# Second layer of a gated feed-forward block: a seven-product form over pairs of quad pairs in two of three passes

## The chip, the cores and the metric

One core of a Trainium2 chip runs the whole program. The metric is device time in microseconds (us), the median of repeated runs; less is better. Line numbers (L1168 and so on) are those of the kernel before, unless it says "of the changed kernel".

## What is computed

Three layers in a row on 2304 tokens of width 512: pooled attention, a mixture of eight experts, and a gated layer. The change touches the gated layer only:

```python
def _moe2_ref(x, w_gate, w_val, w_out):       # x: 2304 x 512, w_gate and w_val: 512 x 1536, w_out: 1536 x 512
    g = x @ w_gate
    silu = g * (1.0 / (1.0 + np.exp(-g)))
    val = x @ w_val
    return (silu * val @ w_out).astype(np.float32)
```

The multiplication by `w_gate` and `w_val` is called the first layer here, that by `w_out` the second.

## The kernel before

**Numbers.** Each operand of a matmul is split into a high part, rounded to the matmul's input type, and a low part, the rest. One product is then three matmuls: high by high, high by low and low by high (`mm3`, L117 to L119, and L1168 to L1170 in the second layer).

**Passes and quads.** Tokens are worked on in three passes of `TB` = 768 (two halves of `HB` = 384). The loop over `m` at the end of the program is the gated layer: 18 steps, six for each pass (`SP2` = 6), and each step takes 256 of the 1536 hidden columns. A step has two calls of `quad`, one with gate weights and one with value weights. A quad is the 256 hidden columns by 768 tokens of the first layer in a form of Strassen's: seven products M1 to M7 of two halves each, so 42 matmuls of 384 columns, in the order M1, M2, M5, M6, M7, M4, M3. Their sums are taken in part in PSUM: M1, M6, M7 and M4 add up in one tile `a` (named `aps`), M5 and M3 in `c` (`cps`), M2 is in `b` (`bps`). After M1, M6 and M7 the running sum in `a` is copied out by ScalarE (ACT, `part_sum`, L1097), and the next product then adds on to the same tile. VectorE (DVE) makes the four blocks 11, 22, 21 and 12 of the result from these copies.

**Second layer.** Before, a step's gated block (silu times value, split in high and low by `value_sink`) is multiplied with the 256 rows of `w_out` by `second_tile`: six token tiles for each step, six matmuls of 512 columns for each tile, into `yps`. They are not run at once: the tiles of step m are queued in `ys` and handed out by `fill_y` within the two quads of step m + 1, three to each, two of them between M6 and M7 and one between M7 and M4. DVE adds each tile to an accumulator in `AC` (L1663); in the sixth step of a pass the tile is then stored. After the last step six tiles are left, and end the program.

**Who sets the order.** The program is written in the order in which it is to run; each engine takes its instructions in that order and waits on semaphores. `quad` calls `after` behind each product: it runs what is in `late` (work of the next engine in a chain), the product's sink, the tasks put at that point (`tasks`) and one step of `side`. PSUM has eight banks: before, in this stage, two for `a`, one for `b`, two for `c` and three for `yps`.

**Rows of w_out.** They are split in high and low once, in the first pass, stored in DRAM (`rows_d`) and fetched by a DMA of GpSimd's queue (POOL) in the later passes, twelve times 1 MB (`split_rows`, L853).

The expert stage ahead of this one already has its second layer as seven products over pairs of quads (`block`, into `mbs`, 128x384 matmuls). Its blocks stand at several points of each quad, among them between M6 and M7 (`at_block`).

## Time and profile before

| | us |
|---|---|
| median of 3 runs | 1985.78 |
| lowest and highest run | 1985.34, 1986.54 |
| the profiled execution's own time | 1986.16 |
| its span, first to last instruction | 1984.5 |

The profile is of one execution, so a sum made from its rows is set against 1986.16, which is 0.38 us over the median. PE is TensorE's matmuls, PEld its weight loads, SPq the queue that issues most DMAs. A matmul's row lasts longer than the stretch to the next matmul's start, because matmuls are pipelined: what one costs in a stream is read as the distance from start to start. Columns of the rows below: a row of the timeline is start and length in us, engine, line, operation, output and input tile, shapes, and in brackets the idle time before it and who ended it. A row of stretches is the stretch, its length, the busy us (and instructions) of PE, PEld, DVE, ACT and POOL, the granted clock as a share of 2.4 GHz, the busy share of the DMA engines and GB/s. A row of groups is line, engine, operation, tiles, shapes and count, then busy us and mean ns of one, then the idle time before them. The gated layer lies from about 1570 us to the end, its passes two and three from about 1705 us.

### The profile page before, as it was taken

How to read it: one execution, taken by the hardware profiler on the slowest of the kernel's cores; microseconds unless marked ns; L12 is line 12 of the kernel's file. 1: busy time of each engine (PE TensorE's matmuls, PEld its weight loads, DVE VectorE, ACT ScalarE, POOL GpSimd, SP SyncE). 2: the span in 40 equal slices, each digit the busy share in tenths (PEclk: the TensorE clock that was granted, in tenths of full speed). 3: DMA queues.
4: the chain of work that ended last, by engine and by line, in shares of the span. 5: the costliest groups of instructions: out<-in, count | busy, mean ns of one | idle time of the engine just before them, and what ended most of it. 6: DMA issues, size and time to landing. Idle time of an engine off the chain costs nothing.

```text
span 1984.5 us, 31152 instructions
## 1 busy us (share of the span) xinstructions
PE 1964.2 (99%) x11081; PEld 1871.4 (94%) x11081; DVE 1421.9 (72%) x2257; ACT 885.8 (45%) x1709; POOL 1310.0 (66%) x1173
## 2 busy tenths in 40 slices
PE   8999999999999999999999999999999999999999
PEld 7899888999999899999999999999999999999998
DVE  7763868777777868877777788777776855656555
ACT  4453544444444444443444434444444554544543
POOL 7674567888887466867667667677675766445442
PEclk9999999999999999999999999999999999999999
DMA  7674677888888899989989899898888564543542
GB/s 195 183 210 117 218 274 267 311 292 311 312 304 307 295 315 320 330 300 313 313 306 316 292 309 330 312 312 310 314 318 284 174 239 149 201 161 138 173 146 85
DMA packets 217227, 513.82 MB, mean 259 GB/s; under 512 B 35472, under 2 KB 107760, under 8 KB 210928
## 3 DMA queue, kind: packets, MB, share of 16 engines
q1 hardware_dynamic: 212176, 496.10, 72.8%
q0 software_dynamic: 4896, 15.73, 2.9%
q8 instruction: 88, 1.44, 0.3%
q14 instruction: 67, 0.55, 0.1%
HBM read 360.73 MB, written 151.04 MB: 258 GB/s over the span
## 4 chain that ended last, share of the span: by engine, by line
PE 92%; DVE 4%; DMA 1%; ACT 1%; issue 1%; POOL 1%; SPq 0%; DVEq 0%; POOLq 0%; ACTq 0%
PE aps L119 8%; PE aps L117 8%; PE aps L118 8%; PE mbs L118 7%; PE mbs L117 7%; PE mbs L119 7%; PE yps L1168 6%; PE yps L1170 6%; PE yps L1169 6%; PE cps L117 4%; PE cps L119 4%; PE cps L118 4%; PE bps L117 2%; PE bps L118 2%; PE bps L119 2%; PE mps L360 1%
## 5 line engine op out<-in xcount | busy, mean ns | idle before, releaser
L1097 ACT COPY LF<-aps 128x384 f32<-128x384 f32 x378 | 181.5, 480 | 439.6 <-PE aps L119 437.4
L1329 POOL TENSOR_TENSOR LR<-LF,LR 128x384 fp32r<-128x384 f32 x240 | 261.0, 1110 | 172.7 <-ACT LR L1327 172.6
L117 PE MATMUL mbs<-LR 128*128 128x384 f32 x840 | 283.1, 337 | 0.0
L118 PE MATMUL mbs<-LR 128*128 128x384 f32 x840 | 282.5, 336 | 0.0
L119 PE MATMUL mbs<-LR 128*128 128x384 f32 x840 | 281.9, 336 | 0.0
L1376 DVE TENSOR_TENSOR AC<-mbs,AC 128x768 f32<-128x768 f32 x196 | 187.1, 955 | 131.8 <-PE mbs L119 131.1
L1168 PE MATMUL yps<-LR 128*128 128x512 f32 x576 | 225.7, 392 | 0.2 <-DVE AC L1428 0.2
L1170 PE MATMUL yps<-LR 128*128 128x512 f32 x576 | 225.2, 391 | 0.5 <-DVE LR L1611 0.5
L1169 PE MATMUL yps<-LR 128*128 128x512 f32 x576 | 224.6, 390 | 0.2 <-POOL LR L66 0.2
L846 POOL TENSOR_TENSOR LR<-praw,LR 128x512 fp32r<-128x512 f32 (+1 forms) x130 | 135.9, 1064 | 108.4 <-ACT LR L840 68.5
L846 POOL TENSOR_TENSOR LR<-sums,LR 128x1024 fp32r<-128x1024 f32 x65 | 159.2, 2449 | 68.1 <-ACT LR L840 68.1
L1342 POOL TENSOR_TENSOR LF<-LF 128x384 f32<-128x384 f32 x120 | 129.1, 1075 | 57.2 <-DVE LF L1496 45.4
L118 PEld LDWEIGHTS mbs<-LR 128*128 128x128 f32 x840 | 157.8, 188 | 0.0
L119 PEld LDWEIGHTS mbs<-LR 128*128 128x128 f32 x840 | 157.7, 188 | 0.0
L117 PEld LDWEIGHTS mbs<-LR 128*128 128x128 f32 x840 | 157.6, 188 | 0.0
L1430 DVE SCALAR_TENSOR_TENSOR AC<-yps,pr,AC 128x512 f32<-128x512 f32 x168 | 121.1, 743 | 30.9 <-PE yps L1170 27.0
L1336 ACT COPY LF<-bps 128x384 f32<-128x384 f32 x120 | 57.7, 481 | 185.9 <-DVE bps L1496 182.3
L1346 POOL TENSOR_TENSOR LF<-LF 128x384 f32<-128x384 f32 x120 | 130.5, 1088 | 9.4
L1170 PEld LDWEIGHTS yps<-LR 128*128 128x128 f32 x576 | 108.1, 188 | 24.4 <-DVE LR L1611 1.0
L66 POOL TENSOR_TENSOR LR<-rraw,LR 128x512 fp32r<-128x512 f32 x72 | 99.2, 1397 | 41.1 <-ACT LR L65 37.8
L1168 PEld LDWEIGHTS yps<-LR 128*128 128x128 f32 x576 | 108.2, 188 | 19.1 <-DVE AC L1428 0.7
L1169 PEld LDWEIGHTS yps<-LR 128*128 128x128 f32 x576 | 108.2, 188 | 18.5 <-POOL LR L66 0.6
(320 smaller groups left out, 5743.1 us busy)
## 6 DMA issues: line engine op xcount, KB each, us to landing
LR<-w1s_d SPq DMA_DIRECT2D x210, 512.0 KB
LR<-w2s_d SPq DMA_DIRECT2D x210, 512.0 KB
w1s_d<-LR SPq DMA_DIRECT2D x29, 1792.0 KB
w2s_d<-LR SPq DMA_DIRECT2D x24, 1024.0 KB
w2s_d<-LR SPq DMA_DIRECT2D x90, 256.0 KB
praw<-in_moe_w_dram SPq DMA_DIRECT2D x30, 512.0 KB
rraw<-in_moe_w_dram SPq DMA_DIRECT2D x30, 512.0 KB
LR<-rows_d POOLq DMA_DIRECT2D x12, 1024.0 KB, 7.3
```

What stands on the lines that cost most here:

```text
L117: nc.tensor.matmul(ps, lhsT=wh, rhs=ah, start=start, stop=False, skip_group_check=more)
L118: nc.tensor.matmul(ps, lhsT=wh, rhs=al, start=False, stop=False, skip_group_check=more)
L119: nc.tensor.matmul(ps, lhsT=wl, rhs=ah, start=False, stop=stop, skip_group_check=more)
L846: nc.gpsimd.tensor_tensor(out=lo, in0=src, in1=hi.bitcast(F32), op=ALU.subtract)
L1097: nc.scalar.copy(out=t, in_=ps[:, :HB])
L1168: nc.tensor.matmul(ps, lhsT=hh[:, o:o + P], rhs=wh, start=j == 0, stop=False)
L1169: nc.tensor.matmul(ps, lhsT=hh[:, o:o + P], rhs=wl, start=False, stop=False)
L1170: nc.tensor.matmul(ps, lhsT=hl[:, o:o + P], rhs=wh, start=False, stop=j == 1)
L1329: eng.tensor_tensor(out=lo[:, c], in0=src[:, c], in1=hi[:, c].bitcast(F32), op=ALU.subtract)
L1342: nc.gpsimd.tensor_tensor(out=r_of(q, a), in0=r_of(q, b), in1=r_of(q, a), op=ALU.subtract)
L1346: nc.gpsimd.tensor_tensor(out=r_of(q, a), in0=r_of(q, a), in1=r_of(q, b), op=ALU.subtract)
L1376: nc.vector.tensor_tensor(out=acc_of(m), in0=ps[:, :, :HB], in1=acc_of(m), op=ALU.add)
```

## The change

In passes two and three the second layer gets the seven-product form too, with the tokens stationary.

- Two steps make a pair `j` (six hidden blocks of 256 make three pairs in a pass). The gated blocks 11, 22, 21 and 12 of both steps are kept in fp32 (`r_of`), M1, M3 and M2 take a block as it is (`pair_sink`, `split_b`), the other four take sums (`sum_t13`, `sum_t24` on DVE, `split_t` on ACT and POOL).
- `gated_block` is one of the seven products of a pair: 18 matmuls of 256 columns (three token tiles, two steps, three of a split product) into a tile `mbs` of two banks. DVE adds it to `AC` (768 columns).
- The blocks of pair j stand in the four quads of pair j + 1, seven points in all (`at_gated`): after M7 of each quad, and after M2 of all but the first of the four. The last seven run at the end.
- The weight sets of the seven products are made in pass one (`gated_row_sums` on DVE, `split_gated_sums` on ACT and POOL), stored in `w3s_d`, and streamed by SP, 512 KB a block, three blocks ahead. `rows_d` and its twelve DMAs of POOL's queue are gone.
- From the third step of pass two on, PSUM is two banks for `a`, one each for `b` and `c`, and four for two tiles `mbs`. The six tiles left from pass one are handed out two to a quad, in the first three quads of pass two.
- In pass one the low part of a gate or value set's sums is taken in two POOL instructions of 512 columns instead of one of 1024 (in all three passes of this layer, since `pair_lo` is shared).

```diff
 def pair_lo(i, what):
...
-                        nc.gpsimd.tensor_tensor(out=lo, in0=src, in1=hi.bitcast(F32), op=ALU.subtract)
+                        parts = [slice(0, 2), slice(2, 4)] if j == 2 and i >= NE else [slice(None)]
+                        for c in parts:
+                            nc.gpsimd.tensor_tensor(out=lo[:, c], in0=src[:, c], in1=hi[:, c].bitcast(F32), op=ALU.subtract)
...
-                if p:
-                    nc.gpsimd.dma_start(out=rsets[i].rearrange("p a d -> p (a d)"), in_=rows_d[:, (i - NE) % NG])
...
+        def split_gated_sums():
+            t, w = part_of(10.5, 8 * P, F32).rearrange("p (m f) -> p m f", m=4), gated_row_set()
+            nc.scalar.activation(out=w[:, :, 0], in_=t, func=AF.Copy)
+            for c in range(2):
+                m = slice(2 * c, 2 * c + 2)
+                nc.gpsimd.tensor_tensor(out=w[:, m, 1], in0=t[:, m], in1=w[:, m, 0].bitcast(F32), op=ALU.subtract)
...
+        def pair_sink(gs, q):
+            def sink(name, ps, t):
+                src = whole(name, ps, t)
+                out = gs[name] if name == "12" else src
+                nc.vector.tensor_tensor(out=out, in0=src, in1=gs[name], op=ALU.mult)
+                if name != "12":
+                    weighed[q, name] = src
+                    late.append(lambda: split_b(q, {"11": "M1", "22": "M3", "21": "M2"}[name], name))
+            return sink
...
+        GX = ("M1", "M3", "M2", "M6", "M5", "M7", "M4")
...
+        def finish(p, m, other):
+            V = nc.vector
+            return {"M1": [add_of(V, "M2", "M1"), add_of(V, "M6", "M1")],
+                    "M2": [out_rows(p, "M2", 0, 0)],
+                    "M6": [add_of(V, "M7", "M6"), add_of(other, "M3", "M6")],
+                    "M5": [add_of(other, "M3", "M5"), out_rows(p, "M3", 0, 1)],
+                    "M7": [add_of(V, "M4", "M7"), add_of(other, "M5", "M7"), out_rows(p, "M5", 1, 1)],
+                    "M4": [out_rows(p, "M4", 1, 0)]}.get(m, [])
...
+        def gated_block(v, at_once=False):
+
+            j, m = GORDER[v]
+            w = gated_set(v)
+            ps = pools["mb"].tile([P, 2, 512], F32, tag="mb", name="mbs").rearrange("p a b -> p (a b)")[:, :TB]
+            for a in range(3):
+                y = ps[:, 2 * P * a:2 * P * (a + 1)]
+                for q in range(2):
+                    hh, hl = (h[:, a * P:(a + 1) * P] for h in h_of(q, m))
+                    nc.tensor.matmul(y, lhsT=hh, rhs=w[:, q, 0], start=q == 0, stop=False)
+                    nc.tensor.matmul(y, lhsT=hh, rhs=w[:, q, 1], start=False, stop=False)
+                    nc.tensor.matmul(y, lhsT=hl, rhs=w[:, q, 0], start=False, stop=q == 1)
+            load_gated(v + 3)
+            if j % NGP == 0:
+                nc.vector.tensor_copy(out=rows_of(m), in_=ps)
+            else:
+                nc.vector.tensor_tensor(out=rows_of(m), in0=ps, in1=rows_of(m), op=ALU.add)
...
+        at_gated = {(0, "M7"): 0, (1, "M2"): 1, (1, "M7"): 2, (2, "M2"): 3, (2, "M7"): 4, (3, "M2"): 5, (3, "M7"): 6}
+
+        def pair_tasks(m, x, tasks):
+
+            j = (m - SP2) // 2
+            for (a, point), k in at_gated.items():
+                if a == x and j > 0:
+                    merge(tasks, {point: [lambda k=k: gated_block(7 * (j - 1) + k)]})
+            V, G = nc.vector, nc.gpsimd
+            if x in (0, 2) and (x or j):
+                q = 0 if x else 1
+                merge(tasks, {"M1": [lambda: sum_t13(q, V)], "M2": [lambda: sum_t24(q, V)]})
+            if x == 3:
+                merge(tasks, {"M4": [lambda: split_t(0, "M6", "22", G)], "M3": [lambda: split_t(0, "M5", "11", G)]})
+            if x == 0 and j:
+                merge(tasks, {"M6": [lambda: split_t(1, "M6", "22", G)], "M4": [lambda: split_t(1, "M5", "11", G)]})
...
+            take = 2 if m in (SP2, SP2 + 1) else len(ys) // 2
+            more = deque(ys.popleft() for _ in range(min(take, len(ys))))
...
-            quad(i + 1, ys, tasks, value_sink(gs, hs, n))
+            if p:
+                pair_tasks(m, x + 1, tasks)
...
+            quad(i + 1, more, tasks, pair_sink(gs, g) if p else value_sink(gs, hs, n))
+            if m == SP2 + 1:
+                assert not ys
+                ps_open.close()
+                banks_c[:] = [ps_c]
+                pools["mb"] = ps_open.enter_context(tc.tile_pool(name="ps_mb2", bufs=2, **left))
...
-            ys = deque(second_tile(n, t, hs, done2) for t in range(TT))
+            if p == 0:
+                ys = deque(second_tile(n, t, hs, done2) for t in range(TT))
         while late:
             later()
-        while ys:
-            ys.popleft()()
+        sum_t13(1, nc.vector)
+        sum_t24(1, nc.vector)
+        split_t(1, "M6", "22", nc.gpsimd)
+        split_t(1, "M5", "11", nc.gpsimd)
+        while side:
+            side.popleft()()
+        for k in range(7):
+            gated_block(len(GORDER) - 7 + k, True)
```

PE's order in the gate quad of the last step. `aps` is the tile `a`; T2 is M6's operand, T3 that of M7. Before, two tiles `yps` of six matmuls each stand between M6 and M7; the end of the second of them and M7's start:

```order
L1168 MATMUL yps_18701<-LR_2662 128x512
L1169 MATMUL yps_18701<-LR_2662 128x512
L1170 MATMUL yps_18701<-LR_2662 128x512
L117 MATMUL aps_18653<-T3h_2271,LR_2662 128x384
L118 MATMUL aps_18653<-T3l_2272,LR_2662 128x384
L119 MATMUL aps_18653<-T3h_2271,LR_2662 128x384
```

In the changed kernel, the same quad, M6's second half and M7's start:

```order
L117 MATMUL aps_19030<-T2h_2269,LR_2662 128x384
L118 MATMUL aps_19030<-T2l_2270,LR_2662 128x384
L119 MATMUL aps_19030<-T2h_2269,LR_2662 128x384
L117 MATMUL aps_19030<-T3h_2271,LR_2662 128x384
L118 MATMUL aps_19030<-T3l_2272,LR_2662 128x384
L119 MATMUL aps_19030<-T3h_2271,LR_2662 128x384
```

M7's first matmul is now right behind M6's last one. This is so in 23 quads of the changed kernel, against two of the kernel before.

DVE's order at the end of the program, before: the last products' blocks 21 and 12 (`aps`, `cps`) are multiplied and split, and then the six tiles are added up.

```order
L1606 TENSOR_TENSOR aps_18745<-aps_18745,LF_2661 128x384
L1183 TENSOR_TENSOR cps_18764<-cps_18764,LF_2661 128x384
L1606 TENSOR_TENSOR cps_18764<-cps_18764,LF_2661 128x384
L1611 TENSOR_TENSOR LR_2662<-aps_18745,LR_2662 128x384
L1611 TENSOR_TENSOR LR_2662<-cps_18764,LR_2662 128x384
L1663 TENSOR_TENSOR AC_74<-yps_18835,AC_74 128x512
L1663 TENSOR_TENSOR AC_74<-yps_18844,AC_74 128x512
```

The end in the changed kernel: the last low part (L1357), four sums (L1361, L1365), and then the first of seven `mbs` tiles with the additions of the seven-product form (L1659).

```order
L1636 TENSOR_TENSOR aps_19142<-aps_19142,LF_2661 128x384
L1199 TENSOR_TENSOR cps_19184<-cps_19184,LF_2661 128x384
L1636 TENSOR_TENSOR LF_2661<-cps_19184,LF_2661 128x384
L1357 TENSOR_TENSOR LR_2662<-aps_19142,LR_2662 128x384
L1361 TENSOR_TENSOR LF_2661<-LF_2661 128x384 x2
L1365 TENSOR_TENSOR LF_2661<-LF_2661 128x384 x2
L1691 TENSOR_TENSOR AC_74<-mbs_19267,AC_74 128x768
L1659 TENSOR_TENSOR AC_74<-AC_74 128x768 x2
L1691 TENSOR_TENSOR AC_74<-mbs_19290,AC_74 128x768
L1691 TENSOR_TENSOR AC_74<-mbs_19311,AC_74 128x768
L1691 TENSOR_TENSOR AC_74<-mbs_19333,AC_74 128x768
```

The four sums and two additions of 768 columns now stand ahead of the addition that frees the second `mbs` tile.

## Rows read from the trace of the kernel before

**Rows 1.** the page: busy time of each engine.

```profile
PE 1964.2 (99%) x11081; PEld 1871.4 (94%) x11081; DVE 1421.9 (72%) x2257; ACT 885.8 (45%) x1709; POOL 1310.0 (66%) x1173
```

**Rows 2.** the view of stretches, in the expert stage.

```profile
1200.00:1300.00 100.00, 100.00 (x576) 100.00 (x575) 81.44 (x125) 41.81 (x81) 74.61 (x71) 1.00 0.90 313
```

**Rows 3.** the view of stretches: two steps each, in passes one, three and three.

```profile
1650.50:1695.50 45.00, 45.00 (x237) 41.96 (x237) 26.07 (x46) 23.87 (x46) 28.72 (x19) 1.00 0.49 154
...
1878.00:1924.00 46.00, 46.00 (x244) 43.06 (x243) 26.89 (x48) 20.84 (x42) 18.75 (x15) 1.00 0.40 138
1924.00:1970.00 46.00, 46.00 (x243) 43.05 (x242) 27.45 (x50) 18.57 (x38) 16.66 (x12) 1.00 0.29 104
```

**Rows 4.** the timeline of a value quad: last of M6, tiles, copy, M7.

```profile
1963.98 0.34 PE L119 MATMUL aps<-T2h,LR 128*128 128x384 f32 x1
...
1964.15 0.39 PE L1168 MATMUL yps<-LR 128*128 128x512 f32 x1
...
1964.35 0.48 ACT L1097 COPY LF<-aps 128x384 f32<-128x384 f32 x1
...
1966.88 0.34 PE L117 MATMUL aps<-T3h,LR 128*128 128x384 f32 x1
...
1967.92 0.39 PE L1168 MATMUL yps<-LR 128*128 128x512 f32 x1
```

**Rows 5.** the timeline of PE in an early stage with 128x256 matmuls.

```profile
101.39 0.28 PE L119 MATMUL hps<-xh,wl 128*128 128x256 f32 x1
...
102.47 0.28 PE L119 MATMUL hps<-xh,wl 128*128 128x256 f32 x1
```

**Rows 6.** the timeline of the first expert quad, PE and ACT, M6 to M4.

```profile
215.87 0.34 PE L119 MATMUL aps<-T2h,w 128*128 128x384 f32 x1
...
216.25 0.48 ACT L1097 COPY LF<-aps 128x384 f32<-128x384 f32 x1 [0.19 <-PE aps L119]
...
216.78 0.45 PE L117 MATMUL aps<-T3h,w 128*128 128x384 f32 x1 [0.57 <-ACT LF L1097]
...
217.76 0.34 PE L119 MATMUL aps<-T3h,w 128*128 128x384 f32 x1
...
218.67 0.44 PE L117 MATMUL aps<-LR,w 128*128 128x384 f32 x1 [0.57 <-ACT LF L1097]
```

**Rows 7.** the timeline of a gate quad in pass one, M6 to M7.

```profile
1585.07 0.34 PE L119 MATMUL aps<-T2h,LR 128*128 128x384 f32 x1
...
1585.50 0.48 ACT L1097 COPY LF<-aps 128x384 f32<-128x384 f32 x1 [0.40 <-PE aps L119]
...
1586.03 0.45 PE L117 MATMUL aps<-T3h,LR 128*128 128x384 f32 x1 [0.62 <-ACT LF L1097]
```

**Rows 8.** the timeline at the end: first tile, its wait, last matmul, addition.

```profile
1971.41 0.39 PE L1168 MATMUL yps<-LR 128*128 128x512 f32 x1
...
1972.35 0.40 PE L1169 MATMUL yps<-LR 128*128 128x512 f32 x1
...
1973.29 0.51 PE L1170 MATMUL yps<-LR 128*128 128x512 f32 x1 [0.55 <-DVE LR L1611]
...
1980.22 0.39 PE L1170 MATMUL yps<-LR 128*128 128x512 f32 x1
1980.65 0.69 DVE L1663 TENSOR_TENSOR AC<-yps,AC 128x512 f32<-128x512 f32 x1 [0.67 <-PE yps L1170]
```

**Rows 9.** the page: groups of instructions by line.

```profile
L1329 POOL TENSOR_TENSOR LR<-LF,LR 128x384 fp32r<-128x384 f32 x240 | 261.0, 1110 | 172.7 <-ACT LR L1327 172.6
...
L1376 DVE TENSOR_TENSOR AC<-mbs,AC 128x768 f32<-128x768 f32 x196 | 187.1, 955 | 131.8 <-PE mbs L119 131.1
...
L118 PEld LDWEIGHTS mbs<-LR 128*128 128x128 f32 x840 | 157.8, 188 | 0.0
```

**Rows 10.** the view of lines, expert stage, DVE, shapes apart.

```profile
L1183 DVE TENSOR_TENSOR bps<-cps,LF 128x384 f32<-128x384 f32 x48 | 26.9, 561 | 17.4 <-ACT LF L1097 17.4
...
L1349 DVE TENSOR_TENSOR AC<-AC 128x768 f32<-128x768 f32 x7 | 9.9, 1414 | 0.0
```

More of the change, by code (lines that the diff above doesn't have):

```diff
@@ L1230, in next_weights @@
                 at("M3", lambda: store_rows(n))
+                if not expert:
+                    at("M5", lambda: gated_row_sums(n))
+                    at("M4", split_gated_sums)
             at("M5", lambda: pair_sums(i + 1))
@@ new lines, in fused_kernel, with gated_set, load_gated, rows_of @@
+        NGP = NG // 2
+        GORDER = [(j, m) for j in range((NPASS - 1) * NGP) for m in GX]
+        def gated_set(v):
+            return part_of(60.5 + 4 * (v % 3), 8 * P).rearrange("p (q h f) -> p q h f", q=2, h=2)
+        def load_gated(v):
+            if v < len(GORDER):
+                j, m = GORDER[v]
+                nc.sync.dma_start(out=gated_set(v).bitcast(F32).rearrange("p q h f -> p q (h f)"),
+                                  in_=w3s_d[:, j % NGP, BX.index(m)])
+        def rows_of(m):
+            return AC[:, EX.index(m) * TB:(EX.index(m) + 1) * TB]
@@ new lines, in gated_block @@
+        def gated_block(v, at_once=False):
+            j, m = GORDER[v]
+            w = gated_set(v)
[10 more added lines that the diff above has]
+                nc.vector.tensor_copy(out=rows_of(m), in_=ps)
+            else:
+                nc.vector.tensor_tensor(out=rows_of(m), in0=ps, in1=rows_of(m), op=ALU.add)
+            if j % NGP == NGP - 1:
+                steps = finish(1 + j // NGP, m, nc.gpsimd if at_once else nc.vector)
+                if at_once:
+                    for f in steps:
+                        f()
+                else:
+                    side.extend(steps)
+            later()
@@ new lines, in fused_kernel @@
+        at_gated = {(0, "M7"): 0, (1, "M2"): 1, (1, "M7"): 2, (2, "M2"): 3, (2, "M7"): 4, (3, "M2"): 5, (3, "M7"): 6}
[12 more added lines that the diff above has]
+                merge(tasks, {"M6": [lambda: split_t(1, "M6", "22", G)], "M4": [lambda: split_t(1, "M5", "11", G)]})
+            if j == 0 and x == 3:
+                merge(tasks, {a: [lambda v=v: load_gated(v)] for v, a in enumerate(("M1", "M2", "M5"))})
@@ L1622, in fused_kernel @@
             gs, hs = {}, {}
-            more = deque(ys.popleft() for _ in range(len(ys) // 2))
+            x = l % 2 * 2
+            g = l % 2 if p else 0
+            take = 2 if m in (SP2, SP2 + 1) else len(ys) // 2
+            more = deque(ys.popleft() for _ in range(min(take, len(ys))))
             tasks = last_blocks(0) if m == 0 else {}
@@ L1635, in fused_kernel @@
                 merge(tasks, {"M2": [lambda n=("T1", "T3")[l - 3]: sum_x(n, nc.gpsimd)]})
-            quad(i, more, tasks, gate_sink(gs, m), 2 if m == 1 else 0)
+            quad(i, more, tasks, gate_sink(gs, m, g), 2 if m == 1 else 0)
             tasks = last_blocks(1) if m == 0 else {}
@@ L1649, in fused_kernel @@
                 merge(tasks, {"M2": [lambda n=("T2", "T4")[l - 3]: sum_x(n, nc.gpsimd)]})
-            quad(i + 1, ys, tasks, value_sink(gs, hs, n))
+            if p:
+                pair_tasks(m, x + 1, tasks)
+            more = ys
+            if m in (SP2, SP2 + 1):
+                more = deque(ys.popleft() for _ in range(min(2, len(ys))))
+            quad(i + 1, more, tasks, pair_sink(gs, g) if p else value_sink(gs, hs, n))
[4 more added lines that the diff above has]
+                pools["mb"] = ps_open.enter_context(tc.tile_pool(name="ps_mb2", bufs=2, **left))
             if m == 0:
```

73 lines of the change are left out of this document (45 added, 28 removed).

## The prediction

> **What bounds the kernel now.** I read the page first: PE is busy for 1964.2 of the span's 1984.5 us, the next engine is DVE with 72% [rows 1]. Then the stretches, because a share over the whole run can hide a stage: in passes one and three of the gated layer PE is busy in every us of 45 or 46, at clock 1.00, while ACT has 18 to 24, POOL 17 to 29 and DVE 26 to 27 [rows 3]. So in the changed stage the time is the sum of PE's start-to-start distances, plus what PE waits. A busy PE says little about the rate, so the timeline comes next, for two things: what a matmul of each width costs in a stream, and what stands between dependent products. Last the end of the program, where no other work covers a wait.
>
> **Matmuls removed and added.** The rate is read from starts. In one value quad twelve 512-column matmuls take 1966.88 - 1964.15 = 2.73 us, 0.2275 each, and six of 384 columns take 1967.92 - 1966.88 = 1.04 us, 0.1733 each [rows 4]. The 128 columns between them cost 0.054, so a line through the two forms gives 0.1733 - 0.0542 = 0.119 for 256 columns. An early stage has that form: nine of them, high and low parts mixed as in the new block, from 101.39 to 102.47 us, 0.120 each [rows 5]. I take 0.1195.
>
> Removed: 2 passes x 6 steps x 6 tiles x 6 matmuls = 432 of 512 columns, 432 x 0.2275 = 98.3 us. Added: 2 x 3 pairs x 7 products x 18 = 756 of 256 columns, 756 x 0.1195 = 90.3 us. The changed order has these counts (PE's rows grow by 324 = 756 - 432), so the change does what it says: seven eighths of the columns. The gain is **-8.0 us** and not an eighth of 98.3, because each matmul has some 12 ns that don't depend on its width, and there are more of them.
>
> **The uncovered copies.** M1, M6, M7 and M4 add up in one tile `a`, and ACT must copy `a` out before the next of them may write it. Before, two tiles `yps` stand between M6 and M7: the copy starts at 1964.35, 0.2 us behind the first tile's start, is done in 0.48 us, and M7 starts at 1966.88 without a wait [rows 4]. The change hands out its blocks after M2 and after M7, none after M6. The order shows M7 right behind M6 in 21 quads more than before: all 20 from the third step of pass two on, and the value quad of the second step, whose tiles have been used up. That quad also has nothing between M7 and M4. So 22 uncovered copies.
>
> The trace has such places. In the first expert quad the last of M6 starts at 215.87, the copy runs from 216.25, M7 starts at 216.78. The sixth matmul of M7 starts at 217.76; six undisturbed distances from 215.87 would be 216.91, so it costs 0.85 us (0.74 of wait, and about 0.11 because the first matmul after a wait is slower). M7 to M4 in the same quad is the same 0.91 from start to start [rows 6]. A gate quad of pass one, with ACT as loaded as here, has 1586.03 - 1585.07 = 0.96, a loss of 0.79, with the slow start 0.90 [rows 7]. I take 0.85: 22 x 0.85 = **+18.7 us**; bounds 22 x 0.74 = 16.3 and 22 x 0.95 = 20.9. Nothing covers it: PE takes its matmuls in order, and the wait is for the very tile it writes next. ACT is free when M6 ends (its blocks of work there, 0.5 us each, are released one or two products earlier), so I add no queueing.
>
> **The end.** Before, the six last tiles lose time once: 0.94 from 1972.35 to 1973.29, instead of 0.23, and the next 0.1 more; this goes, **-0.8**. After the last quad the new order has 7 x 18 x 0.1195 = 15.1 us of PE (counted above). Put the end of M3 at 0. DVE first finishes block 12 and the last low part (0.2 + 4 x about 0.5, done near 2), then four sums of 384, bounded below by 0.56 of the same width [rows 10] less what a read from PSUM costs, near 0.5, and above by 0.7: done near 4.2. Only then it frees the first `mbs` tile (0.96 [rows 9]): 5.2. The third block wants that tile at 4.3, and starts 0.9 late. Two additions of 768 stand next on DVE, at most 1.41 each (the row of such additions with POOL at work [rows 10]), near 1.2: 7.6; then the second tile, 8.5, wanted by the fourth block at 7.4: another 1.1. The low parts for the fourth block (ACT, then POOL with 1.11 each [rows 9]) come near 6 to 7 and are not late. So **+2.1**, bounds 0 (if the sums are done by 3.3) and 3.5. The last addition is 768 wide instead of 512 (0.96 against 0.69 [rows 8, 9]) and the last store is 384 KB beside a second one, instead of 256 KB: **+0.8**, bounds 0.3 and 1.5.
>
> **What I cost at nothing.** In pass one each step gets four additions of 256 on DVE, one ACT copy of 1024, two POOL low parts and a store in seven pieces; there DVE has 19 of 45 us free, ACT 21, POOL 16 [rows 3], and no matmul of pass one reads the result. In passes two and three SP gets 42 loads of 512 KB, each waiting for PE to finish a block, with the loads of the next weights queued behind. Three sets make a load two blocks early, at least 4 us; the DMA engines are busy for 0.29 to 0.49 there [rows 3]. Without that cover a block would wait 2 to 3 us, so up to +3 at the end, where blocks are back to back. POOL loses twelve DMA issues and gets eight low parts of 1.11 for each pair of steps: some 9 us in 48, beside 17 to 19 in 46. One `c` bank instead of two: M5 of the next quad waits for block 12. Behind a gate quad that takes three more hops (ACT, DVE), but there a block of 2.15 us stands after M2; behind a value quad it is done 1.4 us after M3, and M1 and M2 take 2.1. The expert stage lives with the same banks and has PE busy for 100 of 100 us [rows 2]. The range gets 0 to +4 for all this.
>
> **Sum.** -8.0 + 18.7 - 0.8 + 2.1 + 0.8 = +12.8. The profiled execution took 1986.16, which gives 1999.0; it is 0.4 over the median of the runs, so I say **1998.6 us**. Own bounds: -8.4 + 16.3 - 0.8 + 0 + 0.3 + 0 = +7.4, and -7.6 + 20.9 - 0.8 + 3.5 + 1.5 + 4 = +21.5.
>
> **A rule.** In the trace a weight load lasts 188 ns [rows 9], longer than the 120 ns from one 256-column matmul to the next [rows 5], so loads run under earlier matmuls and under each other. The Trainium skill, page "TensorE: Matmul & The Clock Gate", section "The mechanism", says that a weight load overlaps matmuls in flight only where it goes to another group of rows of the array. By that rule a load would stand between any two matmuls, and narrower ones would pay it more often; the trace disagrees, with its 120 ns. It stays as a rival below.
>
> **Rivals.** (1) **The copies are covered after all, and the kernel is faster.** The place is M6 to M7. Without the 18.7 the sum is -5.9, so 1979.9 us. The point from which it decides: (8.0 - 2.1) / 22 = 0.27 us for each copy. For it: PE's order leaves ACT free at that moment. Against: the copy alone takes 0.48, and all three places in the trace give 0.74 or more [rows 6, 7]. (2) **No change that can be measured**: the narrow matmuls run at their columns alone, 256 / 2.4 GHz = 0.107 us, 756 x 0.0125 = 9.5 us less, so 1989.1. Against: neither form in the stage does so [rows 4], nor did the early one [rows 5]. (3) **More waits, much slower**: with one `c` and one `b` bank and DVE in strict order, half of the 20 quads wait another 1 us behind a block's addition (0.96) at M2 or M5: +10, so 2009. For it: margins of 0.7 to 0.9 us in quads without a block after M2. Against: rows 2. (4) **Weight loads pace the blocks**: 756 x (0.188 - 0.1195) = +52, so 2051; against it stand rows 5.
>
> **How the numbers follow.** Forecast 0.80, rivals 0.05, 0.06, 0.07 and 0.02. A measurement of this kernel tells about 0.2% (4 us) from no change. Slower by more: 0.80 + 0.07 + 0.02 = 0.89; within: 0.06; faster by more: 0.05. The range holds the forecast's own bounds, 1993 to 2007, cut above where all upper ends would have to meet, and widened a little below for copies that come out shorter: 1991 to 2006. That leaves out the rivals, 2 in 10.
>
> **What will show it.** Right: in the changed profile M7's first matmul in each quad of the last 250 us waits for ACT's copy of `aps`, some 0.6 us of idle, 22 times more than before, and this group heads PE's waits; new blocks have starts 0.12 us apart; in the end the third and fourth block wait for DVE. Wrong: starts of M6's last and M7's first matmul less than 0.45 us apart, a rate of the blocks clearly off 0.12, or a larger wait than that for ACT's copy, for DVE at M2 and M5 or for a weight load.

## The result, and the profile after

| | before | after |
|---|---|---|
| time, median of 4 runs each | 1985.67 us (1985.34 to 1986.54) | 2016.05 us (2015.67 to 2017.45) |
| span of the profiled execution | 1984.5 us | 2014.0 us |
| PE, busy | 1964.2 us [rows 1] | 1965.8 us |

The changed kernel is slower: ratio 1.015, 95% interval 1.0138 to 1.0162. The prediction was 1998.6 us with a range of 1991 to 2006; direction and main mechanism hold, but the loss is more than twice the forecast. The engines' busy time on the page after answers [rows 1]:

```profile
PE 1965.8 (98%) x11405; PEld 1881.1 (93%) x11405; DVE 1494.9 (74%) x2310; ACT 909.8 (45%) x1751; POOL 1391.4 (69%) x1260
```

PE has 324 matmuls more, and its share fell by a point only. The stretches tell more. The columns are those of [rows 3] (PE, PEld, DVE, ACT, POOL busy; granted clock; DMA share; GB/s); the first three stretches are those of [rows 3], the last two are short ones behind long waits:

```profile
1650.50:1695.50 45.00, 44.15 (x233) 41.10 (x232) 35.83 (x55) 23.99 (x45) 33.08 (x26) 1.00 0.49 163
1878.00:1924.00 46.00, 42.89 (x275) 41.30 (x275) 32.53 (x51) 22.69 (x46) 24.64 (x23) 1.00 0.59 198
1924.00:1970.00 46.00, 44.05 (x290) 43.01 (x288) 28.74 (x48) 22.99 (x45) 26.19 (x24) 1.00 0.49 165
1846.00:1852.00 6.00, 4.84 (x25) 4.84 (x26) 4.39 (x7) 4.98 (x9) 4.29 (x4) 0.72 0.00 0
1994.00:2003.00 9.00, 7.94 (x53) 7.94 (x54) 7.27 (x8) 1.58 (x2) 6.14 (x5) 0.81 0.49 158
```

PE is no longer busy in every us: 2 to 3 us of 46 are idle in pass three, and 0.85 of 45 in pass one, which the forecast left untouched. DVE rose from 26 to 36 us of 45 in pass one. The clock of 0.72 and 0.81 is a mean between the two levels of 2.4 and 1.2 GHz; before, it was 1.00 in the first four, as in this one, and the program had ended ahead of the fifth:

```profile
1846.00:1852.00 6.00, 6.00 (x33) 5.64 (x32) 3.26 (x7) 2.68 (x6) 1.24 (x2) 1.00 0.66 218
```

The six largest groups of PE's waits from the start of the gated layer's pass one (line and releaser, us in total, times, longest):

```profile
PE aps L117 <- ACT LF L1113: 18.3, 24, 3.1
PE cps L117 <- DVE bps L1199: 5.1, 5, 2.1
PE mbs L1684 <- DVE AC L1691: 1.9, 1, 1.9
PE cps L117 <- DVE LF L1636: 1.0, 1, 1.0
PE mbs L1684 <- DMA LR<-w3s_d: 0.6, 1, 0.6
PE bps L117 <- DVE LF L1607: 0.5, 1, 0.5
```

The first group is the uncovered copy of the prediction: 23 of its 24 are new ([rows 7] is the 24th). Of the others only the third, a stall for DVE at the end, has a term in the forecast; the fifth, a wait for a set of weights at the end, and the rest were forecast at nothing. One ordinary place, a value quad's M6, copy, M7 and first block, against [rows 4]:

```profile
1957.47 0.34 PE L119 MATMUL aps<-T2h,LR 128*128 128x384 f32 x1
1957.85 0.48 ACT L1113 COPY LF<-aps 128x384 f32<-128x384 f32 x1 [1.76 <-PE aps L119]
...
1958.38 0.45 PE L117 MATMUL aps<-T3h,LR 128*128 128x384 f32 x1 [0.57 <-ACT LF L1113]
...
1959.53 0.28 PE L1684 MATMUL mbs<-LR 128*128 128x256 f32 x1
...
1959.65 0.28 PE L1685 MATMUL mbs<-LR 128*128 128x256 f32 x1
```

From M6's last start to M7's first there are 0.91 us, 0.74 more than the undisturbed 0.17, as in [rows 6]. The block starts are 0.12 apart, as forecast from [rows 5].

By the starts of the quads, the time went like this (us). The forecast's terms are put on the stages by their counts: -8.2 + 1.7 for steps 6 and 7 (36 matmuls of 512 columns, two copies), -81.9 + 75.3 + 17.0 for steps 8 to 17 (360 such matmuls, 630 of 256 columns, 20 copies), -8.2 - 0.8 + 15.1 + 2.1 + 0.8 for the end:

| stage | before | after | difference | in the forecast |
|---|---|---|---|---|
| pass one, steps 1 to 5 | 116.3 | 122.0 | +5.7 | 0 |
| steps 6 and 7 | 45.7 | 40.4 | -5.3 | -6.5 |
| steps 8 to 17, to the last M3's end | 228.4 | 246.4 | +18.0 | +10.4 |
| from there to the end | 13.1 | 25.3 | +12.2 | +9.0 |

### The profile page after: what moved, and what is told of

Its sections match the earlier page's. It is cut to its first block, busy times and chain, and to the rows that moved or that the text cites. A ratio compares the mean times of both kernels' runs of the same rounds, so it can differ in the third digit from the quotient of the medians.

```text
span 2014.0 us, 32218 instructions
## 1 busy us (share of the span) xinstructions
PE 1965.8 (98%) x11405; PEld 1881.1 (93%) x11405; DVE 1494.9 (74%) x2310; ACT 909.8 (45%) x1751; POOL 1391.4 (69%) x1260
## 4 chain that ended last, share of the span: by engine, by line
PE 88%; DVE 7%; ACT 2%; issue 2%; DMA 1%; POOL 0%; SPq 0%; DVEq 0%; ACTq 0%; POOLq 0%
PE aps L117 8%; PE aps L119 8%; PE aps L118 8%; PE mbs L117 7%; PE mbs L118 7%; PE mbs L119 7%; PE yps L1184 4%; PE yps L1186 4%; PE yps L1185 4%; PE cps L117 4%; PE cps L119 4%; PE cps L118 4%; PE bps L117 2%; PE bps L118 2%; PE bps L119 2%
## 5 line engine op out<-in xcount | busy, mean ns | idle before, releaser
L1348 POOL TENSOR_TENSOR LR<-LF,LR 128x384 fp32r<-128x384 f32 x288 | 314.7, 1116 | 185.1 <-ACT LR L1346 184.9
L851 POOL TENSOR_TENSOR LR<-sums,LR 128x512 fp32r<-128x512 f32 (+1 forms) x101 | 168.0, 1678 | 23.9 <-ACT LR L843 23.9
L1184 PE MATMUL yps<-LR 128*128 128x512 f32 x432 | 169.5, 392 | 0.5 <-DVE AC L1447 0.5
L1361 POOL TENSOR_TENSOR LF<-LF 128x384 f32<-128x384 f32 x120 | 129.8, 1082 | 57.2 <-DVE LF L1515 45.4
L1186 PE MATMUL yps<-LR 128*128 128x512 f32 x432 | 168.7, 391 | 0.0
L1185 PE MATMUL yps<-LR 128*128 128x512 f32 x432 | 168.3, 390 | 0.0
L1355 ACT COPY LF<-bps 128x384 f32<-128x384 f32 x144 | 69.3, 481 | 217.3 <-DVE bps L1515 183.7
L1346 ACT ACTIVATE LR<-LF 128x768 fp32r<-128x768 f32 x144 | 122.0, 848 | 48.9 <-PE mbs L119 43.2
L1365 POOL TENSOR_TENSOR LF<-LF 128x384 f32<-128x384 f32 x120 | 132.3, 1103 | 9.4
L1199 DVE TENSOR_TENSOR bps<-cps,LF 128x384 f32<-128x384 f32 x126 | 70.8, 562 | 74.8 <-ACT LF L1113 74.5
L66 POOL TENSOR_TENSOR LR<-LF,LR 128x1024 fp32r<-128x1024 f32 x24 | 60.3, 2512 | 69.2 <-ACT LR L65 63.9
L66 POOL TENSOR_TENSOR LR<-rraw,LR 128x512 fp32r<-128x512 f32 x64 | 88.5, 1405 | 28.3 <-ACT LR L65 23.9
```

The lines of the kernel that those rows point to most:

```text
L66: nc.gpsimd.tensor_tensor(out=lo, in0=src, in1=hi.bitcast(F32), op=ALU.subtract)
L851: nc.gpsimd.tensor_tensor(out=lo[:, c], in0=src[:, c], in1=hi[:, c].bitcast(F32), op=ALU.subtract)
L1184: nc.tensor.matmul(ps, lhsT=hh[:, o:o + P], rhs=wh, start=j == 0, stop=False)
L1185: nc.tensor.matmul(ps, lhsT=hh[:, o:o + P], rhs=wl, start=False, stop=False)
L1186: nc.tensor.matmul(ps, lhsT=hl[:, o:o + P], rhs=wh, start=False, stop=j == 1)
L1348: eng.tensor_tensor(out=lo[:, c], in0=src[:, c], in1=hi[:, c].bitcast(F32), op=ALU.subtract)
```

## The experiments

All kernels but the last are edits of one of the two kernels; each ran beside the kernel before, whose medians in these comparisons were 1986.1 to 1986.3 us. "Less" and "more" are against the 2016.05 of the changed kernel, or against the kernel before where that was edited. "Loss" is the distance from one matmul's start to the next above the undisturbed pitch of its width. In the traces step 1 of pass one starts anywhere from 1579.7 to 1582.5 us, so a difference of two spans holds up to 2.7 us from before that point; stages are compared where it matters.

**1. The copy alone, in the kernel before.** Its value tiles are handed out later, so that none stands between M6 and M7.

```
-            quad(i, more, tasks, gate_sink(gs, m), 2 if m == 1 else 0)
+            quad(i, more, tasks, gate_sink(gs, m), 2 if m == 1 or m >= 8 else 0)
...
-            quad(i + 1, ys, tasks, value_sink(gs, hs, n))
+            quad(i + 1, ys, tasks, value_sink(gs, hs, n), 2 if m >= 8 else 0)
```

> The kernel before with one edit: in passes two and three the waiting value tiles are not placed before the third of a quad's seven products' places (M2), so that no whole value tile stands between M6 and M7 in 20 quads; all the products stay. It makes the uncovered copy between M6 and M7 alone, without the gated layer's new second layer. Theory A: such a place costs what it costs in the changed kernel (.74 to .98 us; the prediction took .85): 20 places give 15 to 20 us, some 2002 us. Rival: in the kernel before ScalarE and VectorE are far enough ahead that a copy hides at half that price or that other tiles take up the slack: under 10 us, below 1996.

Measured: 2003.91 us (2002.36 to 2004.77), ratio 1.0091 (1.0074 to 1.0108): 17.8 us more; the profiled spans differ by 16.2. PE's waits from 1742 us on are one group:

```profile
PE aps L117 <- ACT LF L1097: 12.8, 20, 1.3
```

That is 0.81 to 0.89 us for each of the 20 places, net. By the starts of the quads, steps 8 to 17 took 18.4 us longer, 0.92 a place (one, at the start of pass three, lost 1.51), and the end took 0.8 less, because its one stall was gone. The price of the copy (0.85) and its size as the largest term are shown, apart from the new second layer.

**2. A block at M6 instead of M2.** Fifteen copies get a block of 2.15 us as cover.

```
-        at_gated = {(0, "M7"): 0, (1, "M2"): 1, (1, "M7"): 2, (2, "M2"): 3, (2, "M7"): 4, (3, "M2"): 5, (3, "M7"): 6}
+        at_gated = {(0, "M7"): 0, (1, "M6"): 1, (1, "M7"): 2, (2, "M6"): 3, (2, "M7"): 4, (3, "M6"): 5, (3, "M7"): 6}
```

> The changed kernel with one edit: the 15 blocks of gated products that stood at M2 of a quad (three for each pair of columns of the five full pairs) stand at M6, where in the kernel before a whole value tile or nothing stood. Theory A: a block at M6 covers ScalarE's copy of M6's partial sums that M7's eviction needs; each such place now costs .74 to .98 us, so 15 go: 11 to 13 us less; against it, new waits at the places where a gate quad's products now come with nothing between them (10 places of .5 to 1 us): 2008 to 2013 us. Rival: these copies weigh nothing since TensorE is bound elsewhere: 2016 within 1 us.

Measured: 2018.07 us (2015.16 to 2019.78), ratio 1.0158 (1.0143 to 1.0173). Neither theory: the copies went and the time did not. The two largest groups of PE's waits from 1742 us on:

```profile
PE cps L117 <- DVE LF L1607: 8.8, 10, 2.4
PE aps L117 <- ACT LF L1113: 7.1, 5, 3.1
```

15 of the 20 waits for the copy are gone, and 10 new ones stand at M5 (`cps`), for DVE's multiplication of the quad before, which the block at M2 had covered. That there would be 10 was expected; that they cost nearly as much as the copies was not (eight 0.75, one 2.55, one 1.90). Behind the two long ones the granted clock fell too, to 0.63 and 0.59 over 4 us, which cost 1.3 and 1.5 us more. A block hides a wait only where it stands, and seven of them for a pair of steps can't stand at both places.

**3. Half blocks.** Each block of 18 matmuls is issued as two halves of 9, at 14 places of a pair instead of 7, so that M6, M7 and the M2 of three quads all have cover.

```
-        at_gated = {(0, "M7"): 0, (1, "M2"): 1, (1, "M7"): 2, (2, "M2"): 3, (2, "M7"): 4, (3, "M2"): 5, (3, "M7"): 6}
+        at_gated = [(0, "M6"), (0, "M7"), (0, "M4"), (1, "M2"), (1, "M6"), (1, "M7"), (1, "M4"),
+                    (2, "M2"), (2, "M6"), (2, "M7"), (3, "M2"), (3, "M6"), (3, "M7"), (3, "M4")]
...
+                    merge(tasks, {point: [lambda k=k: gated_block(7 * (j - 1) + k // 2, half=k % 2)]})
```

> The changed kernel with one edit: each block of 18 products of 256 columns is issued as two halves of 9, and the halves stand at M6 and M7 of every quad of passes two and three (and at M2 and M4 where the rest is needed), so that something stands between M6 and M7 in all quads but those of the first pair and the last. The products are the same in number. Theory A: the 20 uncovered copies between M6 and M7 (about .8 us each, 16 to 17 us) go, and nothing takes their place: 1998 to 2001 us. Rival: half a block (about 1.1 us) is too short for the copy and the adder that frees the bank, or the waits move to other tiles: 2006 to 2016 us.

Measured: 2004.01 us (2003.33 to 2004.62), ratio 1.0089 (1.0074 to 1.0104): 12.0 less, between the theories. From 1742 us on, the copies have three waits left of 20, but others are there:

```profile
PE mbs L1686 <- DVE AC L1704: 3.1, 1, 3.1
PE cps L117 <- DVE LF L1636: 3.0, 2, 1.9
PE aps L117 <- ACT LF L1113: 2.6, 3, 1.7
PE cps L117 <- DVE LF L1607: 0.8, 1, 0.8
```

The copies can be covered, with no matmul more or less. By the starts of the quads, steps 8 to 17 took 15.2 us less, the end took 1.4 more (its wait for DVE grew from 1.9 to 3.1), and this execution entered step 1 2.6 us later than the changed kernel's. The waits that are left stand at both ends of pass three and are mostly for DVE.

**4. Pass one's sums on GpSimd.** The four additions of weight row halves (L190) leave DVE.

```
-            for f in take_row_sums(nc.vector, rraw[i], part_of(10.5, 8 * P, F32).rearrange("p (m f) -> p m f", m=4)):
+            for f in take_row_sums(nc.gpsimd, rraw[i], part_of(10.5, 8 * P, F32).rearrange("p (m f) -> p m f", m=4)):
```

> The changed kernel with one edit: the four additions that make the sums of weight row halves for the gated layer's second layer (line 190, in steps 1 to 5 of the first pass) go on GpSimd instead of VectorE. In the changed kernel TensorE loses 2.29, 1.24, 1.01 and 1.02 us in steps 1 to 4 of that pass waiting at M3 for VectorE's whole-weight additions (line 1199); the kernel before had one such wait of .45 us. Theory A: VectorE stands behind these four additions (.79 + 1.33 + 1.51 + 1.52 us), so the waits go: 4.5 to 5.5 us less, 2010.5 to 2011.5 us against 2016. Rival: the waits come from GpSimd's and the queues' added work in these steps (halves, stores), which stays: within 1 us of 2016, or longer since GpSimd has more to do.

Measured: 2013.01 us (2011.77 to 2015.34), ratio 1.0135 (1.0118 to 1.0152): 3.0 less. In the changed kernel DVE's order before one of M3's waits in pass one was (timeline, PE, DVE and ACT):

```profile
1636.34 2.06 DVE L190 TENSOR_TENSOR LF<-AC 128x256 f32<-128x256 f32 x1
1638.32 1.52 DVE L190 TENSOR_TENSOR LF<-AC,LF 128x256 f32<-128x256 f32 x1
...
1641.43 0.55 DVE L1199 TENSOR_TENSOR bps<-cps,LF 128x384 f32<-128x384 f32 x1
...
1642.03 0.44 PE L117 MATMUL cps<-LR 128*128 128x384 f32 x1 [0.84 <-DVE bps L1199]
```

M3 overwrites `cps`, which L1199 must read first; L1199 stands behind the sums. In the run pass one's M3 waits fell from five to one, but two waits of M6 for ACT's copy came (waits of PE from 1580 to 1702 us; the third such wait is that of [rows 7]), and ahead of the first of these copies ACT has this split of the sums:

```profile
PE aps L117 <- ACT LF L1113: 2.3, 3, 1.3
PE cps L117 <- DVE bps L1199: 0.4, 1, 0.4
...
1607.51 1.06 ACT L879 ACTIVATE LR<-LF 128x1024 fp32r<-128x1024 f32 x1 [3.92 <-DMA w3s_d<-LR]
```

So DVE's order is the cause of most of pass one's waits, and some 3 of the 5.7 us come back by this edit alone. The forecast of the experiment (4.5 to 5.5) left out that split: by the trace it waits for the store of the set before it, not for the sums, which GpSimd had finished at 1603.8. In the changed kernel the split waited there for the same store (1.68 us), and M6 lost only 0.27, as M3's wait before it had held TensorE up.

**5. Pass three's first sums, later.** In the first quad of each pair the activation sums stand at M5 and M6 instead of M1 and M2.

```
-                merge(tasks, {"M1": [lambda: sum_t13(q, V)], "M2": [lambda: sum_t24(q, V)]})
+                a, b = ("M1", "M2") if x else ("M5", "M6")
+                merge(tasks, {a: [lambda: sum_t13(q, V)], b: [lambda: sum_t24(q, V)]})
...
-                merge(tasks, {"M6": [lambda: split_t(1, "M6", "22", G)], "M4": [lambda: split_t(1, "M5", "11", G)]})
+                merge(tasks, {"M7": [lambda: split_t(1, "M6", "22", G)], "M4": [lambda: split_t(1, "M5", "11", G)]})
```

> The changed kernel with one edit: in the first quad of each pair the additions that make the pair's activation sums (lines 1361 and 1365, VectorE and GpSimd) stand at M5 and M6 instead of M1 and M2, and one split of them at M7 instead of M6. Theory A: at the start of pass three these sums stand in VectorE ahead of the whole-weight addition that the gate's sigmoid, and behind it ScalarE's copy of M6, wait for; TensorE then loses 3.25 us at one place, is granted half the clock in the stretch after it (pitch .21 us instead of .12), and the copies of the first quads take .98 instead of .74 us: some 5 us go, 2011 us (2009.5 to 2013). Rival: the wait comes from the queue on ScalarE itself and stays: 2016 within 1 us.

Measured: 2017.5 us (2016.95 to 2018.65), ratio 1.0157 (1.0142 to 1.0172): 1.4 more. The theory fell, in its first form. The place in the changed kernel, where TensorE loses 3.25 us:

```profile
1841.98 1.19 DVE L733 TENSOR_TENSOR T3l<-xq,T3h 128x768 fp32r<-128x768 f32 x1
...
1843.10 2.64 DVE L1361 TENSOR_TENSOR LF<-LF 128x384 f32<-128x384 f32 x2
...
1845.66 0.55 DVE L1199 TENSOR_TENSOR bps<-bps,LF 128x384 f32<-128x384 f32 x1
...
1846.24 0.49 ACT L1606 ACTIVATE LF<-bps 128x384 f32<-128x384 f32 x1 [2.82 <-DVE bps L1199]
1846.63 0.47 ACT L1113 COPY LF<-aps 128x384 f32<-128x384 f32 x1
...
1847.16 0.44 PE L117 MATMUL aps<-T3h,LR 128*128 128x384 f32 x1 [3.08 <-ACT LF L1113]
```

The copy waits behind the sigmoid on ACT, the sigmoid for L1199 on DVE, and that stands behind the next pass's split (L733) and the sums (L1361). With the sums some places later the copy there is an ordinary one again (longest wait 0.6), as it is in the first quads of the four other pairs (0.79 of loss instead of 0.97 to 1.32), and M3 waits instead:

```profile
PE aps L117 <- ACT LF L1113: 12.5, 21, 0.6
PE cps L117 <- DVE bps L1199: 3.6, 1, 3.6
```

**6. Those sums left out.**

```
-            if x in (0, 2) and (x or j):
+            if x in (0, 2) and (x or j) and m != 2 * SP2:
```

> The changed kernel with one part left out: the four additions that make the activation sums of one quad pair, the one that falls on the start of pass three (lines 1361 and 1365 there, 2.64 + 1.13 us on VectorE; that pair's products then take unsummed activations). Theory A: at the start of pass three VectorE itself is the limit (it is busy without a gap from 1837.6 to 1848.6, and moving these additions by some places only moved the wait), so without them the 3.25-us wait shrinks to that of an ordinary place (.8) and TensorE's half clock after it (1.5 us) goes: 3.5 to 5 us less, 2011 to 2012.5. Rival: ScalarE's queue or the next pass's activations hold the copy there: within 1 us of 2016.

Measured: 2013.07 us (2011.65 to 2015.74), ratio 1.0137 (1.0122 to 1.0152): 3.0 less, the profiled span 2.4; the longest wait for the copy from 1742 us on is 1.1 instead of 3.1. The runs spread over 4 us, so the 3.0, below the forecast 3.5 to 5, is rough. By the starts of the quads, steps 8 to 17 took 3.7 less, and pass one 0.9 more, as the clock fell behind a wait there. DVE's additions at that place, not ACT's queue, hold that copy.

**7. The end in another order.** DVE's first eviction stands between the sums, row additions come later, and the first low halves are DVE's.

```
+        sum_t13(1, nc.vector)
+        gated_block(len(GORDER) - 7)
+        sum_t24(1, nc.vector)
+        gated_block(len(GORDER) - 6, True)
+        split_t(1, "M6", "22", nc.vector)
+        split_t(1, "M5", "11", nc.gpsimd)
+        gated_block(len(GORDER) - 5)
...
```

> The changed kernel with the end in another order: on VectorE the first eviction of a gated block stands between the last pair's two sum steps (lines 1361 and 1365) instead of behind both, the additions of finished rows (line 1659) stand behind the third block's eviction, and the first split's low halves go on VectorE instead of GpSimd. Theory A: the end stalls are VectorE's order alone: the 2.07-us wait at 1995.06 goes, and the half clock behind it (1.6 us): 3 to 4 us less, 2012 to 2013. Rival: the end is paced by the chain of sums, halves and split activations that the sixth and fifth products need, and by the weight sets' loads: 0 to 1.5 us less, 2014.5 to 2016.

Measured: 2014.86 us (2014.1 to 2015.14), ratio 1.0144 (1.0129 to 1.0159): 1.2 less, in the rival's range. In the changed kernel the sums stand ahead of the first eviction, and two row additions between the first and the second; the third block waits:

```profile
1990.42 1.84 DVE L1361 TENSOR_TENSOR LF<-LF 128x384 f32<-128x384 f32 x2
1992.29 1.84 DVE L1365 TENSOR_TENSOR LF<-LF 128x384 f32<-128x384 f32 x2
1994.05 0.95 DVE L1691 TENSOR_TENSOR AC<-mbs,AC 128x768 f32<-128x768 f32 x1
1995.04 2.64 DVE L1659 TENSOR_TENSOR AC<-AC 128x768 f32<-128x768 f32 x2
...
1995.06 0.39 PE L1684 MATMUL mbs<-LR 128*128 128x256 f32 x1 [1.91 <-DVE AC L1691]
```

With the new order PE's last matmul comes 16.8 us after the last M3's end instead of 19.5: the wait of 1.91 and the half clock behind it go, as theory A said, and one of 0.9 for DVE comes later. But then 7.2 us pass to the end instead of 5.9, for the row additions on POOL came only 1.3 us earlier with it (POOL's last work in the timeline of the run; its three additions end at 2008.46, PE's last start is at 2006.09, and the chain that ended last goes through them):

```profile
2001.45 7.01 POOL L1659 TENSOR_TENSOR AC<-AC 128x768 f32<-128x768 f32 x3 [2.83 <-DVE AC L1691]
```

2.7 won on PE, 1.3 given back behind it: what paces the end then is neither theory's.

**8. Four edits together**: 3, 4 and 7, and the sums of 6 on GpSimd.

```
+                E = G if m == 2 * SP2 else V
+                merge(tasks, {"M1": [lambda: sum_t13(q, E)], "M2": [lambda: sum_t24(q, E)]})
```

> The changed kernel with four edits together: the blocks in halves at M6 and M7 (alone 12.0 us less), the sums of weight row halves on GpSimd (alone 3.0 less), the activation sums at the start of pass three on GpSimd, and the end in the other order. Theory A: each removes its own waits, so they add up: 2016 - 12 - 3 - 4 - 2 = 1995 us (1992 to 1998), still above the 1986 of the kernel before: what then stays are the last blocks behind the last value quad and the waits of VectorE at the passes' ends. Rival: the waits move to the next late engine (GpSimd above all, which two edits load): 2001 to 2005.

Measured: 1999.95 us (1999.73 to 2001.35), ratio 1.0071 (1.0056 to 1.0086). That is between the two ranges: it adds up only in part. GpSimd has a split of the next pass and four low halves (5.34 us) ahead of the sums, so these end late (at 1841.3), and TensorE loses 4.54 us there. The groups of waits are led by

```profile
PE aps L117 <- ACT LF L1113: 4.4, 1, 4.4
```

**9. The same, with these sums behind the crowded stretch.**

```
+            edge = 2 * SP2 <= m <= 2 * SP2 + 1
...
+            if edge and x == 1:
+                merge(tasks, {"M1": [lambda: sum_t13(1, V)], "M2": [lambda: sum_t24(1, V)],
+                              "M6": [lambda: split_t(1, "M6", "22", G)], "M3": [lambda: split_t(1, "M5", "11", G)]})
```

> The run with the four edits together, with one thing otherwise: the activation sums of the quad pair that falls on the start of pass three go back to VectorE, but stand in the value quad after it (at its M1 and M2, their splits at M6 and M3) instead of in the gate quad, where VectorE and GpSimd have the next pass's activations to split. In the run with four edits TensorE lost 4.54 us there behind GpSimd's slower sums and was granted half the clock after it. Theory A: the start of pass three is crowded for some 12 us only, and work that is put behind it costs nothing: 4 to 6 us less, 1994 to 1996 us, still above the kernel before. Rival: what the stretch is short of is VectorE's time altogether, and the wait moves once more, as it did when the sums were put a few places later: 1998 to 2001.

Measured: 1997.4 us (1995.73 to 1997.55), ratio 1.0052 (1.0036 to 1.0069): 2.6 less than run 8 (spans: 2.7), between the ranges of the theories. The 4.54-us loss is gone (the waits for the copy from 1742 us on come to 0.2 us) and the clock stays at 1.00 there; M5's waits of 1.9 and 1.2 at pass three's start and in its second pair stay:

```profile
PE cps L117 <- DVE LF L1636: 3.0, 2, 1.9
...
PE aps L117 <- ACT LF L1113: 0.2, 1, 0.2
```

This is the best version of the change that was run, 18.6 us below it and still 11 above the kernel before. PE's losses from 1490 us on add up to 41.8 us in the changed kernel, 20.8 in this one and 5.0 in the kernel before. If the rest above those 5.0 went as well, its span of 1995.7 would be 1979.9, an estimate: some 5 us under the kernel before. No run shows that it can go.

**10. DVE's additions by themselves.** A kernel of its own: rows of 20 additions, 128x384.

```
    for f in (sbuf_alone, psum_alone):
        for _ in range(20):
            f()
...
    for _ in range(60):
        pool_add()
    for f in (sbuf_beside, psum_beside):
        for _ in range(20):
            f()
```

> A kernel of its own that computes nothing of the reference: 20 VectorE additions of 128x384 with both operands in SBUF and 20 with one operand in PSUM, first with GpSimd idle, then the same 40 beside a row of GpSimd additions of 128x384, no other engine at work; then GpSimd additions alone. In the changed kernel VectorE's additions of that size with both operands in SBUF took .56 to .57 us in the places where GpSimd was idle and .9 to 1.5 where it worked, those with an operand in PSUM .54 to .57 in both. Theory A: GpSimd's work alone makes the difference: .56 us alone, 1.0 to 1.4 beside GpSimd with both operands in SBUF, .56 in both halves with one in PSUM. Rival: the slow ones come from the rest of those stretches (transfers, TensorE's and ScalarE's reads): .56 in all four groups.

Measured, by lines (L45 and L48 with GpSimd idle, L51 and L54 beside it; `ps` is in PSUM, `a` and `b` in SBUF; busy us, mean ns of one):

```profile
L51 DVE TENSOR_TENSOR d<-a,b 128x384 f32<-128x384 f32 x20 | 24.6, 1232 | 0.7
L45 DVE TENSOR_TENSOR s<-a,b 128x384 f32<-128x384 f32 x20 | 11.1, 557 | 0.7
L48 DVE TENSOR_TENSOR s<-ps,b 128x384 f32<-128x384 f32 x20 | 11.1, 557 | 0.7
L54 DVE TENSOR_TENSOR d<-ps,b 128x384 f32<-128x384 f32 x20 | 11.1, 557 | 0.7
```

Theory A holds: beside GpSimd's additions a DVE addition takes 2.2 times as long if both operands are in SBUF, and no ns longer if one is in PSUM.

## Why the prediction was right and wrong

The terms, in us, with what the two traces show for each:

| term | forecast | measured |
|---|---|---|
| matmuls removed and added | -8.0 | -8: undisturbed blocks took 2.15 = 18 x 0.1195, the older forms kept their pitches |
| late copies | 22 x 0.85 = 18.7 | 23 with 21.4 of loss, and about 0.1 each for the slow start after a wait: 23.7 |
| waits for DVE in passes two and three | in 0 to 4 | 1.21 + 0.39 + 0.71 = 2.3 |
| pass one | in 0 to 4 | 5.7 |
| stalls for DVE at the end | 2.1 (0 to 3.5) | 2.1 |
| wait for a set of weights at the end | in 0 to 4 | 0.8 |
| half clock behind two long waits | none | 1.5 + 1.6 = 3.1 |
| last addition and store | 0.8 (0.3 to 1.5) | 1.6 |
| the old end's stall | -0.8 | -0.8 |

They add up to +30.5; the changed kernel entered step 1 1.1 us earlier, less than the scatter of that point, which leaves 29.4 of the 29.5 between the spans. The three rows "in 0 to 4" shared that one allowance and took 8.8.

**Right.** The matmuls' gain is to the tenth; so are the reasons (pitches of 0.2275, 0.1733 and 0.1195, no pacing by weight loads, so rivals 2 and 4 are out). 21 of the 23 copies lost 0.73 to 0.99, mean 0.80, so some 0.9 with the slow start, against the 0.85 taken with it; run 1 shows the price alone. Rival 1 is out as the kernel stands; run 3 shows that it was no law of the kernel but a matter of where the blocks stand.

**Wrong, first step: "ACT is free when M6 ends, so I add no queueing".** It is free in 16 places of 23 (losses of 0.73 to 0.79). In five the copy stands some 0.2 us behind another instruction of ACT (0.94 to 0.99); one of these is no uncovered place at all, but has a tile as cover, at the start of pass two. In two the copy stands on ACT behind a sigmoid that waits long for DVE. One lost 1.32 us, in the third step of pass two, where the pair's sums (L1361) stand in DVE's order ahead of the addition that the sigmoid needs:

```profile
1744.20 2.15 DVE L1361 TENSOR_TENSOR LF<-LF 128x384 f32<-128x384 f32 x2
...
1746.85 0.49 ACT L1606 ACTIVATE LF<-bps 128x384 f32<-128x384 f32 x1 [2.10 <-DVE bps L1199]
```

The other lost 3.25, at the start of pass three, where DVE also splits the next pass's activations. Run 6 shows that the sums on DVE make the second; run 5, that sums put later free both copies, but at pass three's start only move the wait to M3. The rows that I took for ACT were of the middle of pass three, where the queue is short.

**Wrong, second step: "What I cost at nothing", pass one.** "No matmul of pass one reads the result" is true and beside the point. The sums stand in DVE's order ahead of the addition that frees M3's bank, and PE waits for that. Idle time of DVE in the mean (19 of 45 us) is no cover in a strict order. [Rows 10] held a second warning: additions with both operands in SBUF took 1.41 us on average there, against 0.56 for the narrower form that reads PSUM. I used it as an upper bound at the end and did not apply it to pass one, whose sums took up to 2.06 us at 256 columns. Run 4 took 3.0 us away. These five steps still took 118.9 us in it, against 116.3 before; 2.1 of the 2.6 are the two copies behind the split that waits for a store (losses of 1.44 and 0.61), and the cause of the rest stays open.

**Wrong, third step: the end.** The third block's wait is there, 2.07 instead of 0.9, since the four sums took 3.7 us, 0.92 each, above the 0.7 set as their upper bound: two of the three that ran beside GpSimd took 1.25 us each. Nor is there a gain from leaving out a read from PSUM, which the forecast took off 0.56: run 10 has 557 ns with and without it. The fourth block's wait did not come, as the third had been slowed, so that the stalls for DVE sum up to the forecast's 2.1 is luck. What no term held is the clock: after the wait the block took 3.75 us instead of 2.15, at 0.81 granted over 1994 to 2003. In run 7 neither that wait nor a half clock is there, and it shows that PE's side is not the only limit: 1.3 of 2.7 us were given back by additions behind it.

**The range.** Its upper end was cut from 2007 to 2006 because "all upper ends would have to meet", but uncut it would have been passed by some 9 us as well. The bounds themselves were too low: 20.9 for copies that took 23.7, 4 for the waits costed at nothing, which took 8.8, and no term for the clock, 3.1. Pass one, pass three's start, M5's waits and the end all hang on one engine in strict order, DVE, which the change gave 73 us more work. Rival 3 named that engine, with the right direction, at 2009 and 0.07; its places (M2 and M5) held only 2.3 us of it.

## What to carry over

A fine-grained filler can replace a large one only if it stands at the same places: before counting the work it saves, list what each piece it replaces was covering, and check that every such place still has something. Idle time of an engine in the mean is no cover for work on it; look at what stands behind the new work in its order, above all at stage edges, where other extra work gathers. Waits that hang on one engine come late together, and their upper bounds have to be read where that engine is crowded: here even the sum of the bounds was too low.

## What the runs showed of the hardware

**Two operands in SBUF against one in PSUM.** In the changed kernel all of DVE's operations of 128x384 that read PSUM took 0.55 to 0.57 us on average, whatever GpSimd did, while the sums of the same size (L1361, both operands in SBUF) had a mean of 0.79 and went from 0.55 to 1.37 (view of lines, DVE, 1705 to 2014 us):

```profile
L1361 DVE TENSOR_TENSOR LF<-LF 128x384 f32<-128x384 f32 x24 | 19.0, 790 | 0.4
...
L1199 DVE TENSOR_TENSOR cps<-cps,LF 128x384 f32<-128x384 f32 x24 | 13.4, 559 | 1.7 <-PE cps L119 1.7
```

Run 10 shows the cause: 1232 ns beside GpSimd, 557 without it. The Trainium skill, page "SBUF — State Buffer", section "Who interferes with whom", says it beforehand: a DVE instruction with two inputs in SBUF contends with a GpSimd instruction that reads SBUF, one with a single input there does not. Run 10 agrees, with 1232 and 557 ns. The change adds sums within SBUF, and many of them stand where GpSimd is busy.

**The granted clock fell behind two waits, but not behind every such wait.** In the changed kernel it was 0.72 over 1846 to 1852 us, behind a wait of 3.08, and 0.81 over 1994 to 2003, behind one of 1.91. 31 narrow matmuls there had starts 0.21 to 0.22 us apart instead of 0.12, and the blocks behind the two waits took 3.64 and 3.75 us instead of 2.15. Each of these waits cost some 1.5 us more than itself. In run 9, whose first wait is not there, the clock over the same part of the work (1840 to 1860 us) was 1.00. But it is no fixed price: in run 7 the same place waited for 3.06 us and the clock stayed at 1.00, and the wait of 2.13 in pass one, which left it at 1.00 in the changed kernel, was followed by 0.57 in run 6 (stretches of runs 7 and 6, 4 us each):

```profile
1849.00:1853.00 4.00, 3.98 (x28) 3.98 (x29) 3.16 (x5) 3.60 (x6) 3.42 (x3) 1.00 0.00 0
...
1593.50:1597.50 4.00, 3.91 (x13) 3.91 (x14) 2.48 (x5) 2.78 (x5) 1.55 (x2) 0.57 0.78 241
```

What decides it no run here shows, so the 3.1 us in the table belong to that execution.
